# Transposes ahead of the first matmul, and widening moved from the end of attention into the first block

## The chip, the core and the metric

The kernel runs on one core of a Trainium2 chip. The metric is the device time of one execution in microseconds. The engines are TensorE (PE; PEld is its weight loading), VectorE (DVE), ScalarE (ACT), GpSimd (POOL) and SyncE (SP), which only issues transfers. Each has its own queue of instructions and works through it in order; semaphores join them.

## What is computed

Linear attention with random features, then two mixing layers. Cut to what matters:

```python
# attention: phi(x) = exp(h - max h) / sqrt(m),  h = x @ omega.T - |x|^2 / 2
kv = einsum('bhsm,bhsd->bhmd', phi(k), v);  z = sum_s phi(k)
x = einsum('bhsm,bhmd->bhsd', phi(q), kv) / (einsum('bhsm,bhm->bhs', phi(q), z) + 1e-6)
# first layer: mixing over the 576 tokens, then a channel MLP of 1536 units
u = x + (relu(x.T @ w_tok1) @ w_tok2).T
x = u + relu(u @ w_ch1) @ w_ch2
# second layer: Fourier mixing, a norm, an MLP of 2048 units
u = x + real(fft(fft(x, axis=1), axis=2))
out = u + relu(norm(u) @ ff1) @ ff2
```

There are 4 x 576 = 2304 tokens of 512 channels and 8 heads. The weights of the layers arrive as 64-bit numbers. VectorE takes each apart into two single-precision parts, high and low (`widen`), and every matmul of these layers is made of three, high x high, high x low and low x high.

## The kernel before

**Attention** walks 72 slots, each one half of a tile of 128 tokens, keys or queries, and seven more in which the last tiles drain (`attention`, slots n = -1 to 78). In slot n, TensorE projects half n (`project`, L506, three matmuls of 256 columns twice), adds the features of half n-3 to a head's sum (`kv_add`, L540) or turns them (`turn`, L565); later come numerators (`numer`, L582), quotients (`divide`, L595 to L602) and the turned x (`turn_x`, L616). A batch that is complete adds ten pieces of token mixing to the list `fill` (`tok_mix`: two of 15 matmuls, L667, eight of 6 matmuls, L680, whose sums VectorE adds to x2 in L683). One piece is taken from `fill` per slot. Slot 72 opens the buffers of the MLP (`enter_mlp`); slots 72 to 74 split the first operand (`ch_split`, L762 and L763) and issue the first 12 matmuls of the first block (`up`, L776).

**PSUM.** Banks of tag H (two) and A (four). Once the last key sum is done, the list `spare` makes every A request take A, A, H in turn; it is cleared after attention. Tag S then takes two banks that the numerators had.

**Widening** is work on the side. Each chunk (four of token weights, then 12 slabs of the channel MLP, then 16 of the second MLP) has a load into `stg`, seven VectorE operations (L341 take, L352, L356, L360, L364, L368, L372) with one on ScalarE (L348), and a store of the result, `cvo`, to `kept` in DRAM. Two chunks' buffers alternate, so a `cvo` is written again two chunks later, when its store has landed. `weave` writes the order of all of them in one list; each operation has a cost in us, and `Side.step` adds a budget to a credit and takes operations from the list while the credit covers them. The budget of a slot is 0.45 up to slot 35 and 1.2 (SLOT_US) from 36; that of a step of the first block is 3.9 (FIRST_US).

**The first block** (`ch_block`, `mlp`, L864 on) covers 512 tokens in 12 steps, one slab each: step i issues up(i) (12 matmuls into an H bank), `relu` (L860 on ScalarE, L861 on VectorE), then down(i-1) (12 matmuls into four A banks, L898), one piece of `fill`, and a step of widening. The rest of `fill` is emptied ahead of the last down. Slabs come back from `kept` by `mix`, an object that hands out slots: two from slot 72 on, three more after attention, five more (wc0 to wc3, wd) after the first block, when the token mixing's buffers are closed. It fetches in the order of use (0 to 11, then 11 to 0 in the second block, L738 on SP's queue), and a slot is taken from the slab whose next use is farthest off. After attention the loads and stores of widening go by POOL's queue.

Four more blocks of the channel MLP, the Fourier mixing and the second MLP follow; the change leaves them as they are.

Of the kernel before, what the change touches and what calls it, by code (L numbers as in the profile page):

```python
# [9 lines left out]
F32 = mybir.dt.float32  # L10
# [10 lines left out]
B, H, S, D, M = 4, 8, 576, 64, 128  # L21
# [4 lines left out]
NCH, NFF = DCH // 128, DFF // 128  # L26
BLK = 512

NWB = 3
NBLK = (NTOK + BLK - 1) // BLK  # L30

BLOCKS = [0, NBLK - 1, *range(1, NBLK - 1)]

SLOT0_US, SLOT1_US, SLOT_US, FIRST_US, SHORT_US, CH_US, FF_US, S_US, SAVED_US = 1.2, 0.45, 1.2, 3.9, 1.2, 4.3, 3.8, 1.6, 4.6


NP = NFF // 2
# [263 lines left out]
def mix_kernel(ctx: ExitStack, tc: tile.TileContext, qt, kt, va, om, w1, w2, wch, wff, t1, t2, out):  # L303
# [9 lines left out]
    ident = const.tile([128, 128], F32, name="ident")  # L313
# [69 lines left out]
    def weave(chunks):  # L383


        items = []
        for i, ((_, done), work) in enumerate(chunks):
            if not i:
                items += [(0.0, chunks[c][0][0]) for c in range(2)] + work[:1]
            items += work[1:6]  # L390
            if i + 1 < len(chunks):
                items.append(chunks[i + 1][1][0])
            if i + 2 < len(chunks):
                items.append((0.0, lambda i=i: side.later(chunks[i + 2][0][0])))
            items.append(work[6])
            items.append((0.0, lambda done=done: side.later(done)))
        return items


    kept = {}  # L400
    whole = set()

    def slab(j):
        def store(st, free):
            kept[j] = dram.tile([128, 2, 1024], F32, name="kept")
            side.queue.dma_start(out=kept[j], in_=st["o"].bitcast(F32))
            whole.add(j)
            free()
        return widen(wch[j].bitcast(I32), 1024, store)
# [34 lines left out]
    spare = []  # L444
# [24 lines left out]
    def projection():  # L469
        act.dma_start(out=om_sb, in_=om)  # L470
        act.mul(out=om_h, in_=om_sb, mul=scale)
        dve.scalar_tensor_tensor(out=om_l, in0=om_sb, scalar=scale, in1=om_h, op0=ALU.mult, op1=ALU.subtract)
# [241 lines left out]
    def enter_mlp():  # L714

        pl.close()
        for name, stack in (("ub", ctx), ("wa", pm)):
            mlp0[name] = stack.enter_context(tc.tile_pool(name=name, bufs=1, reuse_waits="tile"))
        u = mlp0["u"] = operand()
        mix.free.extend((mlp0["wa"], f"wa{i}") for i in range(2))  # L720

        def begin():
            mlp0["hb"] = up(ch_first(0), *u, ch_cols(0))

        early.extend([mix.refill] + [lambda k=k: ch_split(0, u, [k]) for k in range(4)])
        early.extend([mix.refill, begin])


    def turns(n, c):
        return list(range(n)) if c % 2 == 0 else list(range(n))[::-1]  # L730

    def fetch(x, pl_, tag):
        if x in PAIR1:
            t = pl_.tile([128, 4, 2, 256], F32R, tag=tag, name="w")
            sync.dma_start(out=t.bitcast(F32), in_=kept[x][:, 0:4])
        else:
            t = pl_.tile([128, 2, 1024], F32R, tag=tag, name="w")
            sync.dma_start(out=t.bitcast(F32), in_=kept[x])  # L738
        return t

    def wait_whole(x):
# [39 lines left out]
    def attention():  # L781
        tiles = [(kind, i) for kind, i, g in order if g == (kind == "q")]
        at = {t: order.index(t + (int(t[0] == "q"),)) for t in tiles}
        late = {}
        n_all = len(order)

        def at_slot(n, kind):
            return order[n][1:] if 0 <= n < n_all and order[n][0] == kind else None

        def sums(n):  # L790
            if n in late:
                late.pop(n)()
            if (t := at_slot(n - LAG, "k")) is not None:
                parts = list(pieces(t[0] * 128, 128))
                kv_add(*t, parts[0])
                if len(parts) > 1:
                    late[n + 2] = lambda: kv_add(*t, parts[1])

        def queries(n):
            if (t := at_slot(n - LAG, "q")) is not None:  # L800
                turn(*t)
            t = at_slot(n - LAG_X, "q")
            if t is not None and t[1] == 0:
                turn_x(t[0], at_slot(n - LAG_NUM, "q") != (t[0] + 1, 0))
                for b in range(B):
                    if t[0] == last_tile(b):
                        fill.extend(tok_mix(b))

        def results(n):
            if (t := at_slot(n - LAG_NUM, "q")) is not None:  # L810
                numer(*t)
                divide(*t)
                if t[1] == 0:
                    split_x(t[0])

        loads, splits = list(tiles), list(tiles)
        for n in range(-1, n_all + LAG_X):
            while loads and at[loads[0]] <= n + AHEAD_LOAD:
                load(*loads.pop(0))
            if n == n_all:  # L820
                enter_mlp()
            if 0 <= n < n_all:
                project(*order[n])
            sums(n)
            queries(n)
            while splits and at[splits[0]] <= n + AHEAD_SPLIT:
                split_in(*splits.pop(0))
            if 0 <= n < n_all:
                feature(*order[n])
            results(n)  # L830
            if n >= 2:

                side.step(0.0 if n < 6 else SLOT0_US if n < 10 else SLOT1_US if n < 36 else SLOT_US)
            if fill and (len(fill) > 3 or n % 2 == 0):
                fill.pop(0)()
            for fn in early[:3]:
                fn()
            del early[:3]

    ctx.enter_context(tc.manual_schedule())  # L840
    projection()
    side.rest += weave(tok_weights() + [slab(j) for j in range(NCH)]
                       + [w(p_) for p_ in range(NP) for w in (first, second)])
    attention()
# [3 lines left out]
    pools["S"] = ctx.enter_context(tc.tile_pool(name="ps_s", bufs=2, space=PSUM, reuse_waits="tile")), 2  # L848

    side.defer, side.queue = 0, pool  # L850


    hp = pm.enter_context(tc.tile_pool(name="hp", bufs=2, reuse_waits="tile"))
# [7 lines left out]
        dve.scalar_tensor_tensor(out=hl, in0=hb[:, 0:n], scalar=0.0, in1=hh, op0=ALU.max, op1=ALU.subtract)  # L861
        return hh, hl

    def mlp(steps, first_of, u, cols, down, budget, prepare, twice=False):  # L864


        prev = None
        for i, x in enumerate(steps):
            hb = mlp0.pop("hb") if "hb" in mlp0 else up(first_of(x), *u, cols)
            h = relu(hb, cols)  # L870
            last = i == len(steps) - 1
            if last:
                for fn in prepare[:1]:
                    fn()
            elif twice:
                side.step(budget / 2)
            if prev is not None:
                down(*prev)
            prev = i, x, h
            if not last:  # L880
                if fill:
                    fill.pop(0)()
                side.step(budget / 2 if twice else budget)
        for fn in prepare[1:]:
            fn()
        down(*prev)

    def ch_block(at_, c, u, prepare, budget):
        acc = [bank("A") for _ in range(4)]
        cols = ch_cols(c)  # L890

        def down(n, j, h):
            hi, lo = halves(mix.get(j), 1)
            hh, hl = h
            for c_, (a, v) in enumerate(((hi, hh), (lo, hh), (hi, hl))):
                for i in range(4):
                    cs = slice(i * 128, i * 128 + 128)
                    pe.matmul(out=acc[i][:, 0:cols], lhsT=a[:, cs], rhs=v, start=(n == 0 and c_ == 0),  # L898
                              stop=(n == NCH - 1 and c_ == 2))
            mix.used()  # L900
        mlp(turns(NCH, at_), ch_first, u, cols, down, budget, prepare)
        for i in range(4):
            for off, n, b, s in pieces(c * BLK, cols):
                dve.tensor_tensor(out=x2[b][:, i, s:s + n], in0=acc[i][:, off:off + n], in1=x2[b][:, i, s:s + n],
                                  op=ALU.add)

    u = mlp0["u"]
    u2 = operand()
    def mixed():
        while fill:  # L910
            fill.pop(0)()

    ch_block(0, 0, u, [lambda: (mixed(), ch_split(BLOCKS[1], u2))], FIRST_US)
    u = u2
    pt.close()
    xu = ctx.enter_context(tc.tile_pool(name="xu", bufs=1, side="right", reuse_waits="tile"))
    c2 = ctx.enter_context(tc.tile_pool(name="c2", bufs=1, side="right", reuse_waits="tile"))

    pw = ExitStack()
    wc = pw.enter_context(tc.tile_pool(name="wc", bufs=1, side="right", reuse_waits="tile"))  # L920
    mix.free.extend((wc, f"wc{i}") for i in range(4))
    wd = pm.enter_context(tc.tile_pool(name="wd", bufs=1, reuse_waits="tile"))
    mix.free.append((wd, "wd"))

    def leave_slots():
        mix.leave(wc)
# [671 lines left out]
```

## Time and profile before

| | us |
|---|---|
| median of 3 runs | 944.12 |
| lowest, highest | 944.02, 945.76 |
| profiled execution, whole time | 946.03 |
| its span, first to last instruction | 943.9 |
| TensorE busy in the span | 930.4 (99%) |
| VectorE, ScalarE, POOL busy | 633.2, 306.4, 120.7 |

All rows are of the profiled execution. Start times are in us from the start of its span. A busy TensorE is not one at its peak: the ends of matmuls are modelled, so it is the distance between starts that tells the rate. The granted clock is 1.00 at 2.4 GHz and 0.50 at 1.2 GHz.

### The profile page before, as it was taken

The numbers are of one execution on the slowest core, as the hardware profiler recorded it, in microseconds if no ns is written. First come the engines' busy times: TensorE is split into PE (matmuls) and PEld (weight loads), VectorE is DVE, ScalarE is ACT, GpSimd is POOL, SyncE is SP. The second block draws the span as 40 slices with busy tenths as digits, with TensorE's granted clock in tenths as the row PEclk, the third lists the DMA queues.
The fourth block names the chain that finished last, engine by engine and source line by source line (L and its number), as shares of the span: only waits on it lengthen the run. The fifth ranks groups of instructions, "written<-read, shape, count | busy, mean of one in ns | idle before, by whom it ended". The sixth has DMA issues, their size and how long they took to land.

```text
span 943.9 us, 14085 instructions
## 1 busy us (share of the span) xinstructions
PE 930.4 (99%) x5344; PEld 830.1 (88%) x5344; DVE 633.2 (67%) x1259; ACT 306.4 (32%) x709; POOL 120.7 (13%) x110
## 2 busy tenths in 40 slices
PE   7999999989999999999999999999999999999998
PEld 7999999978889888888888888889999998899986
DVE  5987999886776787877853667666565557533342
ACT  5886777721212322212221122222311113311121
POOL 3353444221211132011000000000000000000000
PEclk9999999999999999999999999999999999999999
DMA  7765554687897586583145358739766656677764
GB/s 268 231 211 177 184 213 160 252 301 258 345 411 318 174 310 236 180 302 135 60 174 213 134 185 270 240 112 386 268 229 234 227 190 226 227 263 253 249 213 151
DMA packets 68257, 216.47 MB, mean 229 GB/s; under 512 B 5600, under 2 KB 14432, under 8 KB 54240
## 3 DMA queue, kind: packets, MB, share of 16 engines
q1 hardware_dynamic: 60992, 172.40, 52.3%
q0 software_dynamic: 7056, 43.06, 12.3%
q8 instruction: 42, 0.69, 0.3%
q14 instruction: 23, 0.19, 0.1%
q10 hardware_dynamic: 144, 0.13, 0.0%
HBM read 169.30 MB, written 42.47 MB: 224 GB/s over the span
## 4 chain that ended last, share of the span: by engine, by line
PE 97%; DVE 2%; ACT 0%; DMA 0%; issue 0%; DVEq 0%; ACTq 0%
PE H L776 23%; PE A L898 16%; PE A L1470 14%; PE H L1457 12%; PE A L1264 7%; PE A L506 6%; PE H L540 4%; PE N L582 3%; PE A L565 2%; PE A L667 1%; PE A L680 1%; PE S L1077 1%; PE S L1090 1%; PE S L680 1%; PE H L667 1%; PE S L667 1%
## 5 line engine op out<-in xcount | busy, mean ns | idle before, releaser
L776 PE MATMUL H<-uh,w 128*128 128x512 f32 (+1 forms) x800 | 216.3, 356 | 2.1 <-DVE x L683 2.1
L776 PEld LDWEIGHTS H<-uh,w 128*128 128x128 f32 x800 | 137.3, 190 | 22.6 <-DVE x L683 2.3
L860 ACT ACTIVATE hh<-H 128x512 fp32r<-128x512 f32 (+1 forms) x92 | 49.1, 534 | 268.8 <-PE H L776 268.6
L776 PE MATMUL H<-ul,w 128*128 128x512 f32 (+1 forms) x304 | 114.2, 376 | 0.4 <-DVE ul L763 0.4
L898 PE MATMUL A<-hh,w 128*128 128x512 f32 (+1 forms) x480 | 108.7, 369 | 0.0
L1470 PE MATMUL A<-w2t,b 128*128 128x512 f32 x384 | 99.3, 394 | 0.0
L861 DVE SCALAR_TENSOR_TENSOR hl<-H,hh 128x512 fp32r<-128x512 f32 (+1 forms) x92 | 55.8, 606 | 63.8 <-ACT hh L860 63.7
L898 PEld LDWEIGHTS A<-hh,w 128*128 128x128 f32 x480 | 84.2, 188 | 15.0
L1457 PE MATMUL H<-b,w1t 128*128 128x384 f32 x480 | 91.4, 336 | 0.0
L1457 PEld LDWEIGHTS H<-b,w1t 128*128 128x128 f32 x480 | 85.0, 188 | 4.0 <-DVE tmp L1501 0.3
L1470 PEld LDWEIGHTS A<-w2t,b 128*128 128x128 f32 x384 | 70.6, 188 | 11.7
L524 ACT ACTIVATE f<-A,mx 128x128 f32<-128x128 f32 x240 | 69.8, 396 | 23.2 <-DVE mx L520 22.6
L776 PEld LDWEIGHTS H<-ul,w 128*128 128x128 f32 x304 | 57.6, 190 | 10.1 <-DVE ul L763 0.8
L898 PE MATMUL A<-hl,w 128*128 128x512 f32 (+1 forms) x240 | 59.3, 369 | 0.0
L1264 PE MATMUL A<-w,hh 128*128 128x512 f32 x192 | 50.5, 395 | 0.0
L520 DVE TENSOR_REDUCE mx<-A 128x4 f32<-128x512 f32 x70 | 47.7, 682 | 4.2 <-PE A L506 2.9
L898 PEld LDWEIGHTS A<-hl,w 128*128 128x128 f32 x240 | 42.5, 188 | 7.9 <-DVE hl L861 0.4
L540 PE MATMUL H<-v,f 128*128 128x65 f32 x320 | 40.3, 271 | 0.0
L1462 ACT ACTIVATE b<-tmp 128x384 fp32r<-128x384 f32 x16 | 8.4, 525 | 98.1 <-DVE tmp L1523 98.1
L360 DVE SCALAR_TENSOR_TENSOR cvo<-cvy,cvo 128x1024 int32<-128x1024 int32 (+2 forms) x32 | 39.7, 1241 | 0.5
L1264 PEld LDWEIGHTS A<-w,hh 128*128 128x128 f32 x192 | 34.6, 189 | 6.1
L540 PEld LDWEIGHTS H<-v,f 128*128 128x128 f32 x320 | 39.3, 192 | 0.2 <-DVE kvs L545 0.2
(261 smaller groups left out, 1688.8 us busy)
## 6 DMA issues: line engine op xcount, KB each, us to landing
w<-kept SPq DMA_DIRECT2D x60, 1024.0 KB, 6.5
w2t<-kept SPq DMA_DIRECT2D x55, 512.0 KB, 4.9
w1t<-kept SPq DMA_DIRECT2D x48, 512.0 KB, 5.0
stg<-in_wff_dram POOLq DMA_DIRECT2D x16, 1024.0 KB, 6.8
kept<-cvo POOLq DMA_DIRECT2D x13, 1024.0 KB, 6.4
stg<-in_wch_dram SPq DMA_DIRECT2D x9, 1024.0 KB, 6.3
kept<-cvo POOLq DMA_DIRECT2D x16, 512.0 KB, 7.4
kept<-so SPq DMA_DIRECT2D x16, 512.0 KB, 7.7
```

The lines of the kernel that those rows point to most:

```text
L360: dve.scalar_tensor_tensor(out=st["h"], in0=st["y"].bitcast(I32), scalar=-0x80000000, in1=st["h"], op0=ALU.bitwise_and, op1=ALU.bitwise_or)
L506: pe.matmul(out=pj[:, p_ * 256:p_ * 256 + 256], lhsT=a[:, c, :], rhs=w, start=(n == 0), stop=(n == 2), skip_group_check=True)
L520: dve.tensor_reduce(out=mx, in_=p4, axis=AX.X, op=ALU.max, negate=True)
L524: act.activation(out=f[:, hh], in_=p4[:, hh], func=AF.Exp, bias=mx[:, hh])
L540: pe.matmul(out=kvp[b, g][:, hh * 65:hh * 65 + 65], lhsT=ft["k", i, g][:, hh, :], rhs=src["v", i, int(off > 0)][:, 4 * g + hh, :], start=( ...
L776: pe.matmul(out=hb[:, 0:n], lhsT=w(a, kk), rhs=u[:, kk, 0:n], start=(c == 0), stop=(c == 11))
L860: act.activation(out=hh, in_=hb[:, 0:n], func=AF.Relu)
L861: dve.scalar_tensor_tensor(out=hl, in0=hb[:, 0:n], scalar=0.0, in1=hh, op0=ALU.max, op1=ALU.subtract)
L898: pe.matmul(out=acc[i][:, 0:cols], lhsT=a[:, cs], rhs=v, start=(n == 0 and c_ == 0), stop=(n == NCH - 1 and c_ == 2))
L1264: pe.matmul(out=acc[t], lhsT=a[:, t * 128:t * 128 + 128], rhs=w, start=(n == 0 and c_ == 0), stop=(n == NFF - 1 and c_ == 2))
L1457: pe.matmul(out=to, lhsT=w[:, a, cs], rhs=v[:, q], start=(start and n == 0), stop=(n == 5), skip_group_check=True)
L1470: pe.matmul(out=acc[t], lhsT=h[n // 2][:, t * 128:t * 128 + 128], rhs=w[:, n % 2], start=(begins and n == 0), stop=(ends and n == 2))
```

## The change

- Sixteen transposes of the identity into an H bank are issued first on TensorE; nothing reads them.
- The load of the second chunk of token weights goes behind the first operation on the first chunk (slot 6 instead of 2).
- In slots 72 to 78 the budget of widening is 0.45 instead of 1.2, and `spare` is cleared in slot 72.
- In the first block the budget is 4.4 instead of 3.9, two pieces of `fill` are taken per step instead of one, and once `fill` is empty the five slots are opened at once.
- While the first block and what follows run, a finished slab that the slots ask for next is copied from `cvo` to its slot (`fresh`, POOL's queue) ahead of its store.

```diff
--- before.py
+++ after.py
@@ -27,13 +27,14 @@
 BLK = 512
 
 NWB = 3
+IDLE = 16
 NBLK = (NTOK + BLK - 1) // BLK
 
 BLOCKS = [0, NBLK - 1, *range(1, NBLK - 1)]
 
 
 
-SLOT0_US, SLOT1_US, SLOT_US, FIRST_US, SHORT_US, CH_US, FF_US, S_US, SAVED_US = 1.2, 0.45, 1.2, 3.9, 1.2, 4.3, 3.8, 1.6, 4.6
+SLOT0_US, SLOT1_US, SLOT_US, FIRST_US, SHORT_US, CH_US, FF_US, S_US, SAVED_US = 1.2, 0.45, 1.2, 4.4, 1.2, 4.3, 3.8, 1.6, 4.6
 
 
 NP = NFF // 2
@@ -386,7 +387,7 @@
         items = []
         for i, ((_, done), work) in enumerate(chunks):
             if not i:
-                items += [(0.0, chunks[c][0][0]) for c in range(2)] + work[:1]
+                items += [(0.0, chunks[0][0][0])] + work[:1] + [(0.0, chunks[1][0][0])]
             items += work[1:6]
             if i + 1 < len(chunks):
                 items.append(chunks[i + 1][1][0])
@@ -397,12 +398,17 @@
         return items
 
 
-    kept = {}
+    kept, fresh = {}, {}
     whole = set()
 
     def slab(j):
         def store(st, free):
             kept[j] = dram.tile([128, 2, 1024], F32, name="kept")
+            if mlp0.get("direct"):
+                fresh[j] = st["o"]
+                whole.add(j)
+                mix.refill()
+                del fresh[j]
             side.queue.dma_start(out=kept[j], in_=st["o"].bitcast(F32))
             whole.add(j)
             free()
@@ -735,7 +741,10 @@
             sync.dma_start(out=t.bitcast(F32), in_=kept[x][:, 0:4])
         else:
             t = pl_.tile([128, 2, 1024], F32R, tag=tag, name="w")
-            sync.dma_start(out=t.bitcast(F32), in_=kept[x])
+            if x in fresh:
+                side.queue.dma_start(out=t.bitcast(F32), in_=fresh[x].bitcast(F32))
+            else:
+                sync.dma_start(out=t.bitcast(F32), in_=kept[x])
         return t
 
     def wait_whole(x):
@@ -819,6 +828,7 @@
                 load(*loads.pop(0))
             if n == n_all:
                 enter_mlp()
+                spare.clear()
             if 0 <= n < n_all:
                 project(*order[n])
             sums(n)
@@ -830,7 +840,7 @@
             results(n)
             if n >= 2:
 
-                side.step(0.0 if n < 6 else SLOT0_US if n < 10 else SLOT1_US if n < 36 else SLOT_US)
+                side.step(0.0 if n < 6 else SLOT0_US if n < 10 else SLOT1_US if n < 36 or n >= n_all else SLOT_US)
             if fill and (len(fill) > 3 or n % 2 == 0):
                 fill.pop(0)()
             for fn in early[:3]:
@@ -839,6 +849,9 @@
 
     ctx.enter_context(tc.manual_schedule())
     projection()
+    idle = bank("H")
+    for _ in range(IDLE):
+        pe.transpose(idle[:, 0:128], ident, ident)
     side.rest += weave(tok_weights() + [slab(j) for j in range(NCH)]
                        + [w(p_) for p_ in range(NP) for w in (first, second)])
     attention()
@@ -848,6 +861,7 @@
     pools["S"] = ctx.enter_context(tc.tile_pool(name="ps_s", bufs=2, space=PSUM, reuse_waits="tile")), 2
 
     side.defer, side.queue = 0, pool
+    mlp0["direct"] = True
 
 
     hp = pm.enter_context(tc.tile_pool(name="hp", bufs=2, reuse_waits="tile"))
@@ -861,7 +875,7 @@
         dve.scalar_tensor_tensor(out=hl, in0=hb[:, 0:n], scalar=0.0, in1=hh, op0=ALU.max, op1=ALU.subtract)
         return hh, hl
 
-    def mlp(steps, first_of, u, cols, down, budget, prepare, twice=False):
+    def mlp(steps, first_of, u, cols, down, budget, prepare, twice=False, filled=None):
 
 
         prev = None
@@ -878,14 +892,18 @@
                 down(*prev)
             prev = i, x, h
             if not last:
-                if fill:
-                    fill.pop(0)()
+                for fn in fill[:2]:
+                    fn()
+                del fill[:2]
+                if filled and not fill:
+                    filled()
+                    filled = None
                 side.step(budget / 2 if twice else budget)
         for fn in prepare[1:]:
             fn()
         down(*prev)
 
-    def ch_block(at_, c, u, prepare, budget):
+    def ch_block(at_, c, u, prepare, budget, filled=None):
         acc = [bank("A") for _ in range(4)]
         cols = ch_cols(c)
 
@@ -898,7 +916,7 @@
                     pe.matmul(out=acc[i][:, 0:cols], lhsT=a[:, cs], rhs=v, start=(n == 0 and c_ == 0),
                               stop=(n == NCH - 1 and c_ == 2))
             mix.used()
-        mlp(turns(NCH, at_), ch_first, u, cols, down, budget, prepare)
+        mlp(turns(NCH, at_), ch_first, u, cols, down, budget, prepare, filled=filled)
         for i in range(4):
             for off, n, b, s in pieces(c * BLK, cols):
                 dve.tensor_tensor(out=x2[b][:, i, s:s + n], in0=acc[i][:, off:off + n], in1=x2[b][:, i, s:s + n],
@@ -906,21 +924,20 @@
 
     u = mlp0["u"]
     u2 = operand()
-    def mixed():
-        while fill:
-            fill.pop(0)()
-
-    ch_block(0, 0, u, [lambda: (mixed(), ch_split(BLOCKS[1], u2))], FIRST_US)
+    rooms = {}
+
+    def filled():
+        pt.close()
+        rooms["xu"] = ctx.enter_context(tc.tile_pool(name="xu", bufs=1, side="right", reuse_waits="tile"))
+        rooms["c2"] = ctx.enter_context(tc.tile_pool(name="c2", bufs=1, side="right", reuse_waits="tile"))
+        rooms["wc"] = pw.enter_context(tc.tile_pool(name="wc", bufs=1, side="right", reuse_waits="tile"))
+        mix.free.extend((rooms["wc"], f"wc{i}") for i in range(4))
+        mix.free.append((pm.enter_context(tc.tile_pool(name="wd", bufs=1, reuse_waits="tile")), "wd"))
+
+    pw = ExitStack()
+    ch_block(0, 0, u, [lambda: ch_split(BLOCKS[1], u2)], FIRST_US, filled)
     u = u2
-    pt.close()
-    xu = ctx.enter_context(tc.tile_pool(name="xu", bufs=1, side="right", reuse_waits="tile"))
-    c2 = ctx.enter_context(tc.tile_pool(name="c2", bufs=1, side="right", reuse_waits="tile"))
-
-    pw = ExitStack()
-    wc = pw.enter_context(tc.tile_pool(name="wc", bufs=1, side="right", reuse_waits="tile"))
-    mix.free.extend((wc, f"wc{i}") for i in range(4))
-    wd = pm.enter_context(tc.tile_pool(name="wd", bufs=1, reuse_waits="tile"))
-    mix.free.append((wd, "wd"))
+    xu, c2, wc = (rooms[name] for name in ("xu", "c2", "wc"))
 
     def leave_slots():
         mix.leave(wc)
```

## Rows read from the trace of the kernel before

**Rows 1.** Page, part 4: the chain that ended last, by engine.
```profile
PE 97%; DVE 2%; ACT 0%; DMA 0%; issue 0%; DVEq 0%; ACTq 0%
```

**Rows 2.** Waits of PE, whole span: waiter, releaser, us in total, times, longest.
```profile
PE A L506 <- ACT kh L493: 5.3, 1, 5.3
PE H L776 <- DVE x L683: 2.1, 1, 2.1
PE N L616 <- DVE x L598: 1.0, 1, 1.0
PE H L776 <- DVE ul L763: 0.4, 1, 0.4
```

**Rows 3.** Timeline of PE, start: start us, us, line, out<-in, shape, count.
```profile
6.43 0.42 PE L506 MATMUL A<-om_h,kh 128*128 128x256 f32 x1
6.64 0.41 PE L506 MATMUL A<-om_l,kh 128*128 128x256 f32 x1
...
10.91 1.24 PE L540 MATMUL H<-v,f 128*128 128x65 f32 x8
11.96 0.37 PE L506 MATMUL A<-om_h,kh 128*128 128x256 f32 x1
12.16 0.28 PE L506 MATMUL A<-om_l,kh 128*128 128x256 f32 x1
12.28 0.28 PE L506 MATMUL A<-om_h,kl 128*128 128x256 f32 x1
```

**Rows 4.** Windows of PE: stretch, its us, busy us (instructions), granted clock, DMA share, GB/s.
```profile
6.00:7.00 1.00, 1.00 (x5) 1.00 0.94 354
...
205.00:206.00 1.00, 1.00 (x4) 0.52 0.94 385
```

**Rows 5.** Chain that ended last, 195 to 215 us: start us, us, what.
```profile
195.44 1.13 DVE cvo L364
...
201.19 0.60 DVE cvo L352
...
202.22 4.60 PE H L776 x12
...
210.35 2.74 PE H L776 x12
```

**Rows 6.** Timelines of POOL and ACT, start.
```profile
1.23 0.29 POOL masks.py:199 TENSOR_SCALAR_AFFINE_SELECT ident<-ident 128x128 f32<-128x128 f32 x1
...
6.41 1.29 POOL L494 TENSOR_TENSOR kl<-ks,kh 128x512 fp32r<-128x512 f32 x1 [4.63 <-DVE kh L491]
...
9.36 3.66 ACT L524 ACTIVATE f<-A,mx 128x128 f32<-128x128 f32 x12
```

**Rows 7.** Timeline of PE: four transposes and what follows them.
```profile
33.98 0.60 PE L565 MATMUL A<-ident,f 128*128 128x128 f32 x4
34.42 1.00 PE L582 MATMUL N<-kvs,qpT 128*128 128x65 f32 x8
```

**Rows 8.** Timelines of SP's queue and DVE: token weights, their load and first use.
```profile
9.05 0.91 SPq L330 DMA_DIRECT2D stg<-in_w_dram  x2
...
25.02 0.48 DVE L341 TENSOR_SCALAR cvy<-stg 128x640 f32<-128x640 f32 x1
```

**Rows 9.** Line L421, issues from 256 to 259 us: issue to landing.
```profile
DMA to landing us min/median/max: 12.6/14.2/15.9
```

**Rows 10.** Line L738, issues from 256 to 259 us: issue to landing.
```profile
DMA to landing us min/median/max: 11.3/19.7/28.7
```

**Rows 11.** Windows, all engines: the last two columns are DMA share and GB/s.
```profile
265.00:270.00 5.00, 5.00 (x26) 4.24 (x25) 2.79 (x4) 1.66 (x2) 0.55 (x1) 1.00 1.01 421
```

**Rows 12.** Timelines of DVE and PE near the end of the first block.
```profile
273.45 0.69 DVE L352 TENSOR_SCALAR cvo<-stg 128x1024 int32<-128x1024 int32 x1 [4.93 <-DMA kept<-cvo]
...
274.66 0.68 DVE L861 SCALAR_TENSOR_TENSOR hl<-H,hh 128x512 fp32r<-128x512 f32 x1
...
277.13 1.07 PE L898 MATMUL A<-hl,w 128*128 128x512 f32 x4
```

## The prediction

> **What bounds it now.** I read the chain of work that ended last first: it lies on TensorE for 97% of the span [rows 1]. So an edit can gain only where TensorE waits or runs below its full rate; time taken off another engine counts only if TensorE waited for it. The waits of TensorE over the whole span come next [rows 2]: 5.3 us before the first matmul, then 2.1, 1.0 and 0.4 us, all three near 190 to 202 us, where attention hands over to the first block; the rest is 0.5 us. Elsewhere it issues matmul behind matmul, so the other 740 us should not move.
>
> Third comes the rate. At 6.4 us matmuls of 256 columns follow each other every 0.213 us (6.43 to 6.64), at 12.2 us every 0.118 us (12.16 to 12.28) [rows 3]: the lower level, 1.2 GHz (256 columns in 0.213 us), against the upper one, 2.4 GHz. The granted-clock column shows 1.00 at 6 us all the same [rows 4]; here the spacing is what tells. The second slow place shows in that column: 0.52 from 205 to 206 us, after the 2.1 us pause, and the 12 matmuls of one step take 4.60 us at 202.22 against 2.74 at 210.35 [rows 4, 5].
>
> The chain between 195.4 and 202.2 us names the cause of the last two waits: it runs on VectorE, and five of its pieces are widening operations, 4.8 us together, of which the first (L364, 1.13 us) and the last (L352, 0.60 us) stand in [rows 5]. Short operations that TensorE needs (a quotient x, L598; a sum that frees an H bank, L683) queue behind them.
>
> **The start: 16 transposes.** They need only the identity, done at 1.23 + 0.29 = 1.5 us [rows 6]. Four transposes at the upper level take 0.44 us (33.98 to 34.42), 0.11 each [rows 7]; at the lower level at most twice that, 16 x 0.22 = 3.5 us, so they end near 5.1 us, before the first matmul at 5.3, which waits for ScalarE [rows 2]: no cost. If they let the clock rise, the first projections run at 0.118 instead of 0.213 us. In the rows the clock rose 3.7 us after work resumed at 202.22, and between 5.6 and 6.8 us after the first matmul (it is still slow at 10.91: eight of line 540 take 1.05 us to the next at 11.96) [rows 3, 4]. Counted from 1.6 us that is 5.3 to 8.4 us. Full at 5.3: 24 matmuls x 0.095 = 2.3 us, plus 0.24 on the eight of line 540, less some 0.3 us in which the third tile half must wait for POOL's kl (6.41 + 1.29 = 7.70 us) [rows 6]: 2.2 us. At 8.4: nine of the first twelve stay slow, some 1.45 us are left. I take 1.9. What is late next: ScalarE's exponentials, twelve in a row from 9.36 to 13.02 us [rows 6]; by my count they would be ready 0.3 to 0.6 us before TensorE asks, so the gain holds, narrowly.
>
> The Trainium skill, "TensorE: Matmul & The Clock Gate", section "Part 4: PE-mode transpose", speaks against this edit: it says that transposes don't count as busy time in the same way and don't bring the full clock; by it the start would give 0 and the time would be 941.4. No stretch of this trace has transposes alone, so no row here decides it.
>
> **One load later.** The second chunk of token weights is fetched four slots later, behind what SP's queue holds of the loads of slots 3 to 6. Now both loads go at 9.05 us, and its first use on VectorE is at 25.02 [rows 8]; at 1.6 us a slot it is issued near 15 us and still has ten. Cost 0: the cover is that lead. If it were gone, VectorE would wait for the load at 25 us, the maxima and exponentials behind it would be late by as much, and TensorE with them, 1 us at most by the slack they have.
>
> **Last seven slots.** 7 x (1.2 - 0.45) = 5.25 us of budget go. Walking the list of costs by the planner's rule, three widening operations run there instead of nine, and the 4.8 us on the chain go. The waits of 0.4, 1.0 and 2.1 us then have no cause: a quotient's own operations are short and begin as soon as its numerators stand, so that it should be there when TensorE gets to it; the H bank is also freed by clearing `spare` at slot 72, since sums then take A banks only (four, for two or three short uses a slot). 3.55 us, and with the pause gone the slow step too: 4.60 - 2.74 = 1.86 us. Together 5.4. What is late next is TensorE's own work.
>
> **First block.** The widening moves here: 11 steps at 4.4 instead of 3.9, so five slabs (7 to 11) are finished up to a step later. None is late: with list and budgets, slab 7 is complete in step 1 and used in step 7, slab 11 in step 7 and used in step 11. Two pieces of token mixing per step instead of one only reorder TensorE's work; they empty the list in step 5, so five slots open six steps earlier. TensorE waits for no slab here before [rows 2], so that gains 0.
>
> The cost lies behind it. From step 6 a step is 5.5 us of TensorE with no mixing, and VectorE has some 4.7 us of work in it. Slab 11 is stored in step 7 after its copy, both on POOL's queue, and three slab loads go out on SP's in the same moment: 5 MB and one widening load. VectorE may reuse the buffer only when both have landed. Before, the like burst (five loads, one store) made the two halves of a store land 12.6 and 15.9 us after issue [rows 9], the loads 11.3 to 28.7 [rows 10], at 421 GB/s [rows 11]; VectorE stood 4.93 us, and TensorE not at all, since the part it needed was done (274.66 + 0.68) 1.8 us ahead of its use at 277.13 [rows 12]. In the new order I count VectorE asking for the buffer 7 us after issue and TensorE able to stand a landing of 12.5 to 13 us. 5.3 MB at 421 GB/s are 12.6 us. So 0 if it lands in 10 us, some 0.7 at 13, 3.6 at 15.9. I take 0.8.
>
> The Trainium skill, "DMA: Bandwidth & Descriptors", section "Queues, rings and completion order", says each DMA engine takes turns between queues packet by packet. By that POOL's 2 MB would be done when 4 MB have moved, 10 us, and this term would be 0. The row of 15.9 us, one store against five loads, speaks against it.
>
> **Sum.** Profiled execution: 946.03 us, span 943.9. 946.03 - 1.9 - 5.4 + 0.8 = 939.5. The median of the three runs is 944.12, 1.91 less than the profiled one, nearly the 1.86 us of the slow step; I read it so that the median run had the pauses without the slow clock. Then 944.12 - 1.9 - 3.55 + 0.8 = 939.5 as well.
>
> **Rivals.** (a) Transposes don't raise the clock: 944.12 - 3.55 + 0.8 = 941.4. For it: nothing here shows them alone. Against: they are instructions on the same array, with the same loads of weights beside them. (b) The burst lands as late as the worst store before, 15.9 us: 944.12 - 5.45 + 3.6 = 942.3. (c) No loss at the burst, and the median run did have the slow step: 944.12 - 1.9 - 5.4 = 936.8. (d) The other side: the copy and the store of slab 11 share the engines with the three loads as the worst load did before. VectorE then stops for the buffer, and each us past 15.9 is one of TensorE's, which finds no second operand. At 17.8 us nothing is left of the gain, at 19.7 it is slower than 0.2%, at 23.5 us, 949.9. For it: the load of 28.7 us [rows 10]. Against: that was the last of five in one queue. (e) The pauses come back elsewhere: the banks or ScalarE become late in the last slots and hold TensorE for 2 of the 3.55 us, with no gain at the start: 944.12 - 1.55 + 0.8 = 943.4.
>
> **Chances.** Forecast 0.50 at 939.5; (a) 0.18; (b) 0.13; (c) 0.09; (d) 0.06; (e) 0.04. A measurement of this kernel tells about 0.2%, 1.9 us, from no change: faster is below 942.2, slower above 946.0. Faster: 0.50 + 0.18 + 0.09 and 0.05 of (b), 0.82; within: the rest of (b) and (e), 0.12; slower: (d), 0.06. The range 936.8 to 942.4 runs from (c) to (b) and leaves out (d) and (e).
>
> **What would show it.** Matmuls of 256 columns spaced 0.118 us from the first or soon after it, and the eight of line 540 starting near 9.0 to 9.7 instead of 10.91: the start is right; spacing of 0.213 through 11 us: (a). No wait of TensorE for x, and a granted clock of 1.00 between 190 and 215 us: the last slots are right. VectorE waiting for a store or a copy late in the first block, with TensorE waiting for hl beside it: the burst term, and its size. I would be wrong altogether if TensorE shows waits of more than 1 us at new places between 10 and 190 us, because the earlier start then outruns its producers, or in the second block.

## The result

| | before, us | changed, us |
|---|---|---|
| median of 22 runs each | 945.3 | 949.1 |
| lowest, highest | 943.34, 945.98 | 946.85, 959.09 |
| profiled execution, whole time | 946.03 | 947.08 |
| its span | 943.9 | 945.1 |

The ratio of the medians is 1.0052 (95%: 1.0039 to 1.0064): half a per cent slower, where 0.5% faster was forecast. Both gains that were forecast came about, near their size; the first block took back more than both.

The traces show less than this. The profiled execution of the changed kernel is the second shortest of its 22 runs (947.08; the median is 949.1), and that of the kernel before, at 946.03, is longer than all 22 of its runs. So the two traces differ by 1.05 us where the medians differ by 3.8, and what follows accounts for the 1.05.

**What was gained.** The waits of TensorE in the changed kernel (waiter, releaser, us in total, times, longest):

```profile
PE A L916 <- DVE hl L875: 5.0, 1, 5.0
PE H L854 <- POOL ident masks.py:199: 1.6, 1, 1.6
PE H L785 <- DVE ul L772: 0.4, 1, 0.4
...
PE N L622 <- DVE x L604: 0.2, 1, 0.2
```

Against [rows 2], the 2.1 us for the H bank are gone, and the wait for x has shrunk from 1.0 to 0.2. The 5.3 us before the first matmul show as 1.6, the wait of the transposes for the identity; the projections behind them still wait for ScalarE and begin at 5.44 us, where they began at 5.3 before, so what is gained there is the rate. In the first block now stands one wait of 5.0 us, for hl, the second operand of a step of the first block.

The start, on TensorE's timeline (start us, us, line, out<-in, shape, count):

```profile
1.58 3.67 PE L854 MATMUL H<-ident 128*128 128x128 f32 x16 [1.58 <-POOL ident masks.py:199]
5.44 0.48 PE L512 MATMUL A<-om_h,kh 128*128 128x256 f32 x1 [0.19 <-ACT kh L499]
...
6.39 0.28 PE L512 MATMUL A<-om_h,kh 128*128 128x256 f32 x1
6.51 0.28 PE L512 MATMUL A<-om_l,kh 128*128 128x256 f32 x1
...
9.19 1.11 PE L546 MATMUL H<-v,f 128*128 128x65 f32 x8
```

From 6.39 us on, matmuls of 256 columns stand 0.12 us apart, where before they stood 0.21 apart at that time [rows 3], and the first eight of the feature sums start at 9.19 instead of 10.91. At 166.74 us TensorE is still 1.75 us ahead. Part of that lead is the execution that was profiled: in e5 and e6 below, which have no transposes, the same spacing of 0.12 is there from 8.64 and 9.39 us on, and the feature sums start at 9.95 and 10.22. In e5:

```profile
8.64 0.29 PE L506 MATMUL A<-om_l,kh 128*128 128x256 f32 x1
8.77 0.28 PE L506 MATMUL A<-om_h,kl 128*128 128x256 f32 x1
```

In the ten traces with transposes the spacing is there from 6.2 to 7.4 us on and the sums start between 9.00 and 9.51, about 1.1 us earlier in the mean than in the three without.

**What was lost.** The chain that ended last, in the first block (start us, us, what):

```profile
244.09 17.56 DMA kept<-cvo
...
261.68 0.69 DVE cvo L353
262.37 0.61 DVE cvo L357
...
263.00 1.23 DVE cvo L361
264.23 0.61 DVE hl L875
...
264.89 1.94 PE A L916 x4
266.82 3.61 PE H L785 x12
```

The store of slab 10 takes 17.6 us to land. VectorE stands in front of the buffer that it leaves (7.77 us, below), with hl three operations behind. TensorE begins its last matmuls without hl at 257.93 and then stands 4.98 us:

```profile
261.68 0.69 DVE L353 TENSOR_SCALAR cvo<-stg 128x1024 int32<-128x1024 int32 x1 [7.77 <-DMA kept<-cvo]
```

```profile
257.93 1.97 PE L916 MATMUL A<-hh,w 128*128 128x512 f32 x8
264.89 1.94 PE L916 MATMUL A<-hl,w 128*128 128x512 f32 x4 [4.98 <-DVE hl L875]
```

After the pause the granted clock is down at the lower of its two levels. In the windows of all engines it is the number behind POOL's count, 0.77 and 0.50; DMA share and GB/s follow it:

```profile
264.00:266.00 2.00, 1.11 (x3) 0.92 (x4) 2.00 (x4) 0.00 (x0) 0.00 (x0) 0.77 1.02 430
266.00:268.00 2.00, 2.00 (x6) 1.52 (x6) 2.00 (x3) 0.80 (x1) 1.74 (x2) 0.50 0.85 360
```

The four matmuls at 264.89 take 1.73 us to the next start (0.9 at the full rate) and the twelve behind them 3.65, where the same twelve one step earlier take 2.72. So the pause costs 5.0 us and the low clock 1.8 more.

What was moved in those us? The issues on SP's queue and on POOL's:

```profile
239.76 1.97 SPq L747 DMA_DIRECT2D w<-kept  x4
241.77 0.44 SPq L956 DMA_DIRECT2D t_sb<-in_t_dram  x1
```

```profile
240.93 1.03 POOL L331 DMA_DIRECT2D stg<-in_wff_dram  x1 [6.05 <-DVE cvo L365]
243.57 0.53 POOL L745 DMA_DIRECT2D w<-cvo  x1 [1.60 <-DVE cvo L373]
244.09 0.81 POOL L412 DMA_DIRECT2D kept<-cvo  x1
247.47 0.53 POOL L331 DMA_DIRECT2D stg<-in_wff_dram  x1 [2.57 <-DVE cvo L365]
```

Within eight us four slabs of 1.05 MB and a table of 0.33 MB are asked for on SP's queue, and on POOL's a widening load, the copy of slab 10, its store and the next widening load, 1.05 MB each. Why did SP's four go out at 239.76? SP's queue was held by a store (waiter, releaser, us in total, times, longest; 225 to 245 us):

```profile
SPq L747 <- DMA kept<-cvo: 13.9, 2, 9.0
```

The wait of 9.0 us begins at 230.7 and ends when the store of slab 9, issued at 233.85, has landed after 5.9 us, at 239.71. The first load behind it fetches that slab; the other three, for the new slots, follow within 1.3 us. From the issue of slab 10's store at 244.09 to its landing the DMA engines moved 7.07 MB at 403 GB/s, which is 17.5 us: 3.35 MB for SP's queue, nearly all that was left there, and 3.70 for POOL's. So the store is not held by any one transfer; it lands when nearly all that was asked for in front of it, on both queues, has been moved.

**The account of the two profiled executions.** At up(1), the second step's first matmuls, the changed kernel is 202.22 - 198.19 = 4.03 us ahead, has done one piece of mixing more (0.79 us), and is spared the slow step (4.60 - 2.74 = 1.86) [rows 5]: 6.7 us. The pause and the clock behind it take 6.8, so 0.1 is lost there. The second block then starts at 281.40 instead of 280.98; the matmuls of line 1264 (now 1281) start at 538.8 instead of 538.1, and the span ends 1.2 us later. For that last 1.1 us (1.2 - 0.1) I found no single place. The median run of the changed kernel is 2.0 us longer than this one, and of it there is no trace; its mean granted clock is 0.996 against 0.998, and 0.002 of 945 us is 1.9 us: by this estimate, as rough as the third digit, most of those 2.0 are more time at the low clock.

### The profile page after: what moved, and what is told of

It is laid out like the page before. It is cut to its first block, busy times and chain, and to the rows that moved or that the text cites. A ratio compares the mean times of both kernels' runs of the same rounds, so it can differ in the third digit from the quotient of the medians.

```text
span 945.1 us, 14125 instructions
## 1 busy us (share of the span) xinstructions
PE 932.4 (99%) x5360; PEld 830.8 (88%) x5360; DVE 632.2 (67%) x1259; ACT 305.4 (32%) x709; POOL 119.4 (13%) x112
## 4 chain that ended last, share of the span: by engine, by line
PE 91%; DVE 5%; DMA 2%; ACT 1%; issue 1%; POOL 0%; DVEq 0%; ACTq 0%; POOLq 0%
PE H L785 22%; PE A L916 15%; PE A L1487 14%; PE H L1474 12%; PE A L1281 7%; PE A L512 4%; PE N L588 3%; PE H L546 3%; DMA kept<-cvo 2%; PE A L673 1%; PE A L571 1%; PE S L1094 1%; PE A L686 1%; PE S L1107 1%; PE S L686 1%; PE H L673 1%
## 5 line engine op out<-in xcount | busy, mean ns | idle before, releaser
L916 PEld LDWEIGHTS A<-hl,w 128*128 128x128 f32 x240 | 42.9, 190 | 13.1 <-DVE hl L875 5.4
L349 ACT ACTIVATE cvy<-cvy 128x1024 f32<-128x1024 f32 (+2 forms) x32 | 32.8, 1026 | 26.1 <-DVE cvy L342 26.0
```

## The experiments

The theory: the opening of five slots inside the first block sends loads to the DMA engines just when the copies double the traffic of the finished slabs, and stores land too late for VectorE. The rivals: the larger widening budget, the widening that left the last slots, or either half of the traffic alone.

**e1: the start alone,** on the kernel before.

```diff
-                items += [(0.0, chunks[c][0][0]) for c in range(2)] + work[:1]
+                items += [(0.0, chunks[0][0][0])] + work[:1] + [(0.0, chunks[1][0][0])]
...
+    idle = bank("H")
+    for _ in range(IDLE):
+        pe.transpose(idle[:, 0:128], ident, ident)
```

> The kernel before, with the start alone: the 16 transposes and the second token-weight load later. Theory: the changed kernel's trace shows the first eight of line 540 at 9.19 instead of 10.91 us and is still 1.75 us ahead at 167 us, so this is worth 1.7 us: 943.6 against 945.3, ratio 0.998. Rival: the gain is eaten by a wait for VectorE or ScalarE before 190 us: no difference.

Measured 943.96 against 945.48 us, ratio 0.9989 (0.9979 to 0.9998): -1.5. The waits of TensorE:

```profile
PE H L777 <- DVE x L684: 2.1, 1, 2.1
PE H L845 <- POOL ident masks.py:199: 1.6, 1, 1.6
PE N L617 <- DVE x L599: 1.0, 1, 1.0
PE H L541 <- ACT f L525: 0.6, 1, 0.6
```

The start is worth about what this run was expected to give (1.7), with an interval of 0.2 to 2.0 us. The new wait of 0.6 us for ScalarE's exponentials ends at 23.1 us. It need not be the start's: e6 and e5, which lack the start, have it too (0.7 and 1.1), and the changed kernel has none of 0.2 us or more there.

**e6: one line alone,** on the kernel before.

```diff
                 enter_mlp()
+                spare.clear()
```

> The kernel before, with spare cleared at slot 72 and nothing else. If the H bank alone held the first up of the block back, the 2.1 us and the slow clock go and the 1.0 us stays: 942 to 943. If VectorE's queue is what counts, the next thing that it delays (hl of step 0, the A banks of the first down) takes the place of the wait: 944.5 to 945.5.

Measured 941.77 against 945.49, ratio 0.9957 (0.9939 to 0.9975): -3.7, with all runs between 941.34 and 942.26.

```profile
PE A L506 <- ACT kh L493: 5.3, 1, 5.3
PE N L616 <- DVE x L598: 1.0, 1, 1.0
PE H L540 <- ACT f L524: 0.7, 1, 0.7
```

The wait for the H bank is gone and the granted clock is 1.00 from 195 to 215 us. The wait for x stays, and costs no clock. So the 3.7 are the 2.1 of the bank and the slow step behind it; the widening in the last slots had no part in them.

**e5: both edits of the last slots,** on the kernel before: e6 and the smaller budget.

```diff
                 enter_mlp()
+                spare.clear()
...
-                side.step(0.0 if n < 6 else SLOT0_US if n < 10 else SLOT1_US if n < 36 else SLOT_US)
+                side.step(0.0 if n < 6 else SLOT0_US if n < 10 else SLOT1_US if n < 36 or n >= n_all else SLOT_US)
```

> The kernel before, with the last seven slots alone: budget 0.45 and spare cleared at slot 72. Start and first block are those of before. Theory: the waits of 1.0 and 2.1 us go and with them the slow clock after them; 3.1 us, and 1.9 more in executions that had the slow clock: 940.5 to 942.5 against 945.5. Rival (the widening left out of the slots comes back as a wait in the first block, whose budget is the old 3.9): above 944.

Measured 945.38 against 945.49, ratio 0.9991 (0.9967 to 1.0015): nothing, 3.6 us worse than e6. The rival was right. The profiled execution took 943.6, less than the median.

```profile
PE H L776 <- DMA w<-kept: 2.3, 1, 2.3
PE H L540 <- ACT f L524: 1.1, 1, 1.1
```

The 2.3 us end at 269.38. TensorE in the windows around them (busy us, granted clock, DMA share, GB/s):

```profile
268.00:270.00 2.00, 0.62 (x3) 1.00 1.03 424
270.00:272.00 2.00, 2.00 (x10) 1.00 1.03 433
```

The granted clock stays at 1.00 behind this pause. The 2.1 us of the last slots are gone and the 1.0 us are down to 0.2, but TensorE now waits for slab 11 itself. The widening that leaves the slots is not free to go: in the first block of before it makes the last slabs late.

**e7: the start and e5,** that is the changed kernel with the block of before.

> Start and last slots of the change, first block of before (budget 3.9, one piece of mixing a step, slots opened at the end, no copies). Burst theory: nothing lands late in the block, since SP's queue is held by slab 11; the two gains add up: 1.5 + 4 = 939 to 940.5. Rival: the widening that left the slots is missing in the first block, and TensorE waits for a slab: above 942.

Measured 945.5 against 945.49, ratio 0.999 (0.9969 to 1.0011): the rival again. The chain that ended last:

```profile
250.44 9.20 DMA kept<-cvo
...
259.70 9.42 DMA w<-kept
...
269.16 4.62 PE H L777 x12
```

Slab 11 goes out to DRAM (9.2 us), and its load is asked for only then and takes 9.4 us among five others that land up to 25.5 us after issue. TensorE waits 4.2 us and does the next step at the low clock, 4.62 us. So a TensorE that is earlier at the block needs either its slabs earlier or a way around DRAM; that is what the copies are for.

**e2: three of the five slots handed out after the first block,** in the changed kernel, their first loads by POOL's queue.

```diff
-        mix.free.extend((rooms["wc"], f"wc{i}") for i in range(4))
-        mix.free.append((pm.enter_context(tc.tile_pool(name="wd", bufs=1, reuse_waits="tile")), "wd"))
+        mix.free.extend((rooms["wc"], f"wc{i}") for i in range(2))
+        rooms["wd"] = pm.enter_context(tc.tile_pool(name="wd", bufs=1, reuse_waits="tile"))
...
+    mix.free.extend((wc, f"wc{i}") for i in range(2, 4))
+    mix.free.append((rooms["wd"], "wd"))
+    by_pool.extend(("wc2", "wc3", "wd"))
```

> The changed kernel, but three of the five early slots (wc2, wc3, wd) are handed out only after the first block, and their loads go by POOL's queue, which is held by the stores. The copies of slabs 10 and 11 and the budget of 4.4 stay. Theory (burst): without the three loads at 240 us slab 10's store lands within some 9 us instead of 17.6, TensorE does not wait for hl, and the time is about 945.3 - 1.7 - 4.2 = 939.5. Rival (copies): the copy ahead of the store on the same queue is what delays it; the store still lands after 14 us or more and the time stays above 945. Rival (budget): VectorE asks for the buffer too early whatever the loads do; the time stays above 944.

Measured 940.82 against 945.48, ratio 0.9955 (0.9938 to 0.9971), in four runs: -8.3 from the changed kernel.

```profile
PE A L920 <- DVE hl L879: 0.7, 2, 0.3
```

With one load in place of four on SP's queue the same stores land 12.1 and 13.1 us after issue, not the 9 that were expected, and the wait for hl falls from 5.0 to 0.7 in two pieces. That is without a change of the budget of 4.4, which is therefore not the cause by itself.

**e3: slabs 10 and 11 copied by ScalarE,** in the changed kernel, with the loads where they are.

```diff
-                side.queue.dma_start(out=t.bitcast(F32), in_=fresh[x].bitcast(F32))
+                for h in range(2):
+                    act.copy(out=t[:, h], in_=fresh[x][:, h])
```

> The changed kernel, but ScalarE copies slabs 10 and 11 from cvo to their slots (two of 1024 columns each, some 1.05 us apiece) instead of a transfer: 2 MB less for the DMA engines, the three loads still go at 240 us. Burst: the store still shares the engines with three slab loads and two widening loads, lands after some 13 us, and TensorE waits 1 to 3 us: 943 to 946. Copies: the store lands in 7 us, no wait: 939.5.

Measured 942.62 against 945.48, ratio 0.9982 (0.9964 to 1.0001): -6.5 from the changed kernel. The stores land after 13.3 and 10.7 us, as the burst theory has it. Whether it is the 2 MB less that helps or the copy's place ahead of the store in POOL's queue, this run does not tell.

```profile
PE A L917 <- DVE hl L876: 1.2, 2, 0.7
```

**e8: both, e2 and e3 together.**

> The changed kernel with both cures: the three loads late by POOL's queue, slabs 10 and 11 copied by ScalarE. Burst theory: the store of slab 10 lands in 6 to 8 us, as the stores before it, and TensorE waits for no hl: 939 to 940, 0.7 us better than with late loads alone. Rival: the copies on ScalarE (2.1 us a slab) hold up its relu, TensorE waits for hh: 941 or more.

Measured 939.75 against 945.49, ratio 0.993 (0.9909 to 0.9951), with runs of 938.91 to 940.34. The stores of slabs 10 and 11 land after 10.4 and 5.3 us, nothing in the block holds TensorE, and the granted clock is 1.00 from 190 to 215 and from 258 to 270 us. The whole list of waits of at least 0.2 us begins:

```profile
PE H L859 <- POOL ident masks.py:199: 1.6, 1, 1.6
PE H L790 <- DVE ul L777: 0.4, 1, 0.4
PE S L1115 <- DVE gath L1150: 0.2, 1, 0.2
```

With the changed kernel, e2, e3 and e8 the two causes are told apart, by the medians: neither 939.75; the copies alone 940.82, so +1.1; the early loads alone 942.62, +2.9; both 949.1, +9.4. Each interval is some 1.2 to 2 us to either side, so the small steps are rough, and the large one is not. Each alone nearly fits into the slack that TensorE has, and the two together go past it. (ScalarE's copies take 1.0 us a half there, and e8 shows no wait of TensorE for them.)

**e4: the budget of the first block back at 3.9,** in the changed kernel (`FIRST_US` 4.4 to 3.9).

> The changed kernel with the first block's budget back at 3.9 instead of 4.4. Burst: slab 10 is then stored about a step later, near 250 us, into the same rush of loads of 240 us, which is half done by then, and VectorE asks for the buffer 10 us instead of 8.5 us after: the wait shrinks but stays, 942 to 946. Budget: with 12% less on VectorE per step there is no wait: 939.5 to 940.

Measured 946.97 against 945.48, ratio 1.0026 (1.0011 to 1.0041), above both forecasts. Its profiled execution has the wait for hl at 3.8 us with a store of 16.3 us; it took 953.07, 6.1 over the median of its runs. Most of those 6.1 us lie far from the burst: TensorE waits 1.9 us for ScalarE's exponentials, until 24.0 us, and from 26 to 36 us the granted clock is 0.50.

```profile
26.00:30.00 4.00, 4.00 (x22) 0.51 0.10 19
30.00:36.00 6.00, 6.00 (x30) 0.50 1.03 320
```

By the medians the budget is some 2 us of the loss (949.1 against 946.97), with intervals that just overlap, and the rest is elsewhere.

**e3b: no copies at all,** in the changed kernel (the line `mlp0["direct"] = True` taken out): slabs 10 and 11 come back from DRAM.

> The changed kernel without the copies: slabs 10 and 11 come back from DRAM, as all others. SP's queue is then held by these two loads until their stores land, so the three loads of 240 us go after 260 us. If the three loads in front of slab 10's store are the cause, VectorE's wait shrinks below 4 us; but slab 11's own load falls into the rush, and TensorE waits for w as in the kernel with the old block, 2 to 5 us: 942 to 946. If the copies were the whole cause: no wait, 939.5.

Measured 946.9 against 944.76, ratio 1.0018 (0.9985 to 1.0051).

```profile
PE A L915 <- DVE hl L874: 2.8, 1, 2.8
PE H L785 <- DMA w<-kept: 2.1, 2, 1.4
```

Half of the old loss is still there, and beside it stands the loss of e7, a slab that comes late. The three loads now leave behind slab 11's store and load, between 259.8 and 263.1 us, as expected, and the store that VectorE waits for is one of the second MLP's weights, which lands 16.1 us after issue among them. Taking the copies out does not cure it; taking them off the DMA engines (e3) brings most of the cure.

**e10: the widening back in the last slots,** in the changed kernel (the condition `or n >= n_all` taken out).

> The changed kernel with the budget of 1.2 back in the last seven slots (start, clearing, block at 4.4, two pieces a step, early slots and copies stay). Slab 11 is then stored in step 5 and slab 10 in step 4. Theory: the rush of 240 us stays, but the buffers that it holds are asked for later by VectorE (the store of slab 11 some 12 us after issue), so TensorE waits 0 to 2 us; the quotient's wait of 1 us returns: 941 to 943.5. Rival (the rush alone decides, whatever is stored when): 946 or more.

Measured 949.25 against 944.76, ratio 1.0045 (1.003 to 1.006), in four runs. This was a miss for the theory as I had put it: I held that slabs finished earlier would be stored before the loads came. The chain that ended last:

```profile
235.73 9.21 DMA kept<-cvo
...
252.48 18.76 DMA kept<-cvo
...
272.69 1.76 PE A L916 x4
```

The slabs are stored earlier, but the stores behind them, of the second MLP's weights, 0.52 MB each, now meet the same loads and land after 18.8 and 19.2 us. The loads decide, whichever store is beside them.

**e9: the start and `spare.clear()`,** on the kernel before, nothing else.

> The kernel before with the 16 transposes, the later load and the clearing of spare at slot 72; widening and first block untouched. Theory: the clearing alone gave 941.8, the start alone 1.5 us, and they lie in different stretches: 940.0 to 940.5. Rival: the earlier start shifts the block's transfers and brings a wait for a late slab back: 942 or more.

Measured 940.45 against 944.76, ratio 0.996 (0.9945 to 0.9975), in four runs. TensorE's waits are 1.6 for the identity, 1.0 for x and 0.4 for ul; the clock is 1.00. A few lines of the change, without its first block, beat both kernels. e8 is lower still (939.75, and no wait for x), though the intervals of the two ratios just overlap.

## Why the prediction was wrong

**The bound** was read rightly: every gain and the loss are waits of TensorE or its low clock.

**The start** held in its mechanism, and in size with some luck. 1.9 us were taken; 1.75 are there at 166 us, 1.5 in e1, and e9 is 1.3 under e6. But the rise "between 5.6 and 6.8 us after the first matmul" was read from one execution, and a late one: in e6 and e5 it comes 4.1 and 3.2 us after the first matmul. Rival (a) is refuted: with the transposes in front the clock did rise earlier. The rule of the Trainium skill on which (a) rested ("TensorE: Matmul & The Clock Gate", "Part 4: PE-mode transpose") does not agree with this trace: after 3.67 us of nothing but transposes the projections stand 0.12 us apart from 6.39 us on. The moved load cost nothing, as said; no wait of VectorE or TensorE near 25 us appeared.

**The last slots** held in size, not in cause. 5.4 us were forecast; at up(1) the lead is 6.7, less 1.75 of the start 4.9. But e6 gives 3.7 of it to the one line that clears `spare`; the smaller budget adds the 0.8 of the x wait. The forecast named the clearing as a second way to the same end ("also freed by clearing"); it was the main one.

**The first block: "None is late".** False in itself. In e5 and e7, which have the earlier TensorE and the moved widening without the rest, slab 11 is late by 2.3 and 4.2 us. The step failed because I compared the order of slabs with the order of their uses, step by step, and left out the way between: 9.2 us of store and 9.4 of load among other loads in e7, about three steps of this block together.

**The burst term, 0.8 us: the step that failed.** The mechanism (a store that lands late, VectorE before its buffer, TensorE before hl) and the price of the pause were right; the store was slab 10's and not slab 11's, and the time of the loads was wrong. The forecast let TensorE stand a landing of 12.5 to 13 us. Measured: it ends its other work at 257.93 + 1.97 = 259.90, hl stands 3.2 us after the landing (261.65 to 264.84), so the landing may be at 256.7, which is 12.6 us after issue. By the list a landing of 17.56 us costs some 5.3 us; the pause is 4.98. What it had wrong was the landing, 13 us taken against 17.6, for two reasons. First, I placed the loads by the order of the program, beside slab 11's store in step 7. SP's queue runs ahead of that: it had come to the load of slab 9 at 230.7, waited 9.0 us for that slab's store to land, and issued this load, the three for the new slots and a table between 239.76 and 242.2, ahead of slab 10's copy and store. Second, the bytes: 5.3 MB were counted; between the issue of the store and its landing 7.07 were moved. 5.3 MB at the 421 GB/s of [rows 11] gave 12.6 us; 7.07 MB at 403 give 17.5. And the low clock behind a pause, 1.86 us, which I had counted as a gain in the last slots, I did not count as a cost here; it came to 1.8.

The rule that the forecast weighed here ("DMA: Bandwidth & Descriptors", "Queues, rings and completion order", of the Trainium skill: the queues get turns packet by packet) agrees with this trace in its shares. What was moved from 245 to 258 us, for SP's queue (q1) and POOL's (q0): packets, MB, share of the engines' time.

```profile
q1 hardware_dynamic: 351, 2.61, 52.9%
q0 software_dynamic: 342, 2.54, 48.1%
```

But POOL's load, issued at 240.93, moved nothing before 245.2, while SP's queue moved 1.56 MB. From 245.2 on, POOL's 3.15 MB up to the end of the store would, by my estimate, take 15.9 us at half of the 396 GB/s of those 13 us, to 261.1; the store landed at 261.65. The forecast held a row of 15.9 us against the rule; by the trace the loads' start and their bytes were at fault, not the turns. Why POOL's load began 4.3 us late is not shown.

**The sum,** on the profiled execution, forecast -6.5, measured +1.05: 7.6 us (7.7 by the spans, which the rows give). Of these, rounded, the burst and its clock are 6.0 (6.8 against 0.8), the last slots 0.5, the start 0.15, and 1.1 stay without a place. Rival (d) came nearest, though it had slab 11's store and no low clock in its price, and 0.06 was too small a chance: the row that I set beside it, a load of 28.7 us [rows 10], was set aside as the last of one queue, when what it showed was how long anything may take while five slabs are on their way.

**The two clusters of before** were read rightly. Of the runs of the kernel before beside the experiments, those with a mean granted clock of 0.998 lie between 945.2 and 946.2 us (34 runs), and those with 0.999 or 1.000, but one, between 943.7 and 944.8 (27). I read it so that the slow step is there in some executions and not in others; no trace of this kernel without it was taken, but e5 shows a pause of like length with the clock at 1.00. The median of three in the forecast, 944.12, lies by its time among those without it, the one here, 945.3, among those with it. Two more of these runs took 953.4, at 0.991, as the profiled execution of e4 did.

**Open.** Why times differ so much between executions: the changed kernel spreads over 12 us, and those versions whose traces show no pause over 1.1 us behind the start (e2, e3, e6, e8, e9) over 0.9 to 3.0, but for one run of e3 at 950.1. In the changed kernel the mean clock falls from 0.998 to 0.987 as the time rises. Pauses of varying length at the burst would fit, but e4 shows that a low clock elsewhere adds several us too, and the two runs of 953.4 us suggest the same for the kernel before; only single executions have a trace. Whether the table of 0.33 MB matters was not tried, nor the store ahead of the copy, nor the loads moved by less than a block.

## What to carry to other kernels

A load whose memory is free leaves when its queue comes to it, not where it stands in the program beside other engines' work: place a burst by what its queue waits for, here another store's landing, then add up the bytes that both queues still have to move up to the landing, and divide by the rate that full windows show. A pause of TensorE costs its length and often the low clock behind it, here 2 us more, so count it on both sides of the account. And when an edit has several parts that could each cure a wait, try the smallest alone: one line did the work of a rearranged schedule that had to be paid for elsewhere.

## What was unexpected in the hardware

- Transposes of a 128 x 128 identity, 16 in 3.67 us, are enough that matmuls run at 0.12 us per 256 columns from 6.2 to 7.4 us on (ten traces), instead of from 8.64 (e5), 9.39 (e6) or some time after 10.91 (before).
- The same kind of pause of TensorE does not always lower the clock: pauses of 2.1 (before), 2.8 (e3b), 4.2 (e7) and 5.0 us (changed kernel) were followed by a granted clock of 0.50 for some 3 to 4 us, and one of 1.9 us (e4) for some 10; pauses of 2.3 (e5) and 2.1 us (the first in e10) were not, nor was one of 1.0 us (x, in e6).
- A store of 1.05 MB took 5.3 us (e8) to 17.6 us (changed kernel) to land in the first block, and one of 0.52 MB 19.2 us (e10), with how much else was asked for around it.
- Two queues with work shared the DMA engines evenly (2.61 and 2.54 MB in 13 us of the changed kernel).
